# Batch 0's scores in two parts, and loads that cast on GpSimd's queue, in a fused attention and feed-forward kernel

## The chip, the core and the metric

The kernel runs on one core of a Trainium2 chip, as one program with one launch. The metric is the device time of that core in microseconds (us); smaller is better. A core has a matmul engine (TensorE, PE in the profile, whose weight loads are listed apart as PEld), VectorE (DVE), ScalarE (ACT), GpSimd (POOL), and a sync engine (SP) that issues DMAs. Transfers are issued here from SP's queue and from GpSimd's queue. In the built kernels, each queue gives its DMAs eight completion semaphores in turn: the ninth DMA of a queue waits at its issue until the first has landed, the tenth until the second has, and so on.

## The reference

Attention with a selective bias over 8 batches of 8 heads, 576 positions and 64 values a head, and then a gated feed-forward over the 8 x 576 = 4608 tokens:

```python
scores = np.matmul(q, k.transpose(0, 1, 3, 2)) / sqrt(64)
cum = np.cumsum(np.maximum(s, 0.0), axis=-1)
bias = -(cum[:, :, :, None] - cum[:, :, None, :])
scores = np.where(causal, -1e9, scores + np.minimum(bias, 0.0))
attn = softmax(scores)                  # over the keys
x = (attn @ v).transpose(0, 2, 1, 3).reshape(4608, 512)
g = x @ w_gate                          # 512 x 1536
out = (g * sigmoid(g) * (x @ w_val)) @ w_out
```

All inputs and the output are float32 in HBM; the products are made in bf16.

## The kernel before, in words

**Tiles.** Attention works on half batches of four heads ("hb" 0 to 15). For each, k and q (576 KB each) come in as float32, are cast to bf16, transposed on PE, and copied into `KQ[hb % 2]`, two buffers that two half batches share in turn. Four more rows of `KQ`, the cumulative sums in split precision, come from `HL` by four small DMAs (`aug`, L192); they carry the bias into the score product. A head's scores (five tiles of 128 keys, causal, 1600 columns) go into PSUM, ACT takes their exponential into `pt`, GpSimd sets the diagonal blocks' upper triangle to zero (L391, L396), PE multiplies `pt` with v and a column of ones (L413), DVE divides (L429, L430) into `ot`, and PE's transposes put `ot` into `XT`, the feed-forward's input. V comes in by five DMAs a batch (pieces of 64 numbers, 256 bytes) and is cast into `VT[b % 2]`.

**Feed-forward.** It runs over nine tiles of 512 tokens. A tile has twelve steps of a gate product (L626) and a value product (L641), each four matmuls of 512 columns, and then the down product with `w_out` (L670 in tiles 0 and 1; a seven-product form, L711, from tile 2 on). Tile 0 needs tokens 0 to 511, all of batch 0; tile 1 begins with batch 0's last 64 tokens.

**Order.** The order of the instructions on each engine is written by hand and is the program's order. `first_batch` (L882) puts all of batch 0's attention in front of the feed-forward: eight heads, each with one exponential of 1024 and one of 576 columns, with the preparation of half batch 1 between heads 1 and 2, `av` of heads 0 and 1 after head 6, and the rest after head 7. From then on the feed-forward leads: `ffn_items` yields after each product, n counts these items (1 to 24 are the gate and value products of a tile), `hook` runs extra work at a given n, and `pump` puts attention of the next batch between the items, from n = 6 on in tile 0 (`n0`). A matmul that waits holds up all of PE behind it, and the same holds for every other queue.

**Loads.** SP's queue has s, k and q of half batches 0 and 1, the `aug` copies of half batch 0, V of batch 0 (five DMAs), half batch 2, the `aug` of half batches 2 and 3, half batch 3, V of batch 1, half batches 4 and 5. GpSimd's queue has the `aug` of half batch 1, and the weights, which are cast on the way: `wg`, `wv` in two halves of 768 columns each (first half used by steps 0 to 5 of a tile, second half by steps 6 to 11), and `wo` in two halves. The float32 copies of half batches 2 to 4 and of V of batch 1 are cast on GpSimd (L256, L183). Three float32 buffers each for k and q, and one for V, hold back SP's later loads until they are cast.

Of the kernel before, what the change touches and what calls it, by code (L numbers as in the profile page):

```python
# [12 lines left out]
FP32 = mybir.dt.float32  # L13
# [6 lines left out]
def kernel(  # L20
# [20 lines left out]
    HB = 4  # L41
# [67 lines left out]
    with tc.manual_schedule():  # L109
        loaded = {}  # L110
        SRC = {"q": (q, 0), "k": (k, 1)}
# [53 lines left out]

        def load_v(b, cs):
# [36 lines left out]
        def init_vt(i):  # L203
            nc.gpsimd.memset(VT[i][:, :, :, D : D + 1], 1.0)
            nc.gpsimd.memset(VT[i][64:128, 4, :, 0:D], 0.0)
# [24 lines left out]
        init_vt(0)  # L230
        init_vt(1)
        nc.vector.memset(aug_rows(1, 0), 0.0)
        nc.gpsimd.memset(aug_rows(1, 1), 0.0)
        pads(1)

# [10 lines left out]

        cts = {}
# [100 lines left out]
        scs = {}  # L348

        def score_piece(bh, ci):  # L350
            hb, hh = divmod(bh, HB)
            pair = bh < H
            if ci == 0:
                pts[bh] = PTP[0].tile(
                [128, PTW], BF16, tag="pt", bufs=PTP["bufs"], name="pt"
            )
# [3 lines left out]
            if pair:  # L360
                if ci % 2 == 0:
                    bs = take("w")
                    scs[bh] = bs
                else:
                    bs = scs[bh]
                base = (512, 0, 0, 512)[ci]
            else:
                bs = take()
                base = 0
            o = base  # L370
            n = sum(hi - lo for _, lo, hi in CHUNKS[ci])
            sc = view(bs, 1024 if pair else 512)
# [10 lines left out]
            if not pair or ci % 2 == 1:  # L383
                if pair:
                    c0, W = ((576, 1024), (0, 576))[ci // 2]
                else:
                    c0, W = CHUNK_PT[ci], n
                nc.scalar.activation(pt[:, c0 : c0 + W], sc[:, 0:W], AF.Exp, scale=0.125)  # L388
                give(bs)
            if ci == (1 if pair else 0):  # L390
                nc.gpsimd.affine_select(  # L391
                    pt[:, 1088:1600], pt[:, 1088:1600], pattern=[[0, 4], [1, 128]],
                    compare_op=ALU.is_ge, fill=zreg, base=0, channel_multiplier=-1,
                )
# [86 lines left out]
        def side(h, step, ci):  # L481
            bh = HB * h + step
            if bh == H + 3 and ci == 1:
                for c in range(5):
                    cast_v(1, c, nc.gpsimd)
# [60 lines left out]
        def attn_items():  # L546
            for kk in range(H, BH + 2):
                h, step = divmod(kk, HB)
                if kk < BH:
                    if step == 0:  # L550
                        do_later(NR * 2)
                    if step == 1 and 3 < h + 1 < NPE:
                        cast_one(h + 1, "k", nc.gpsimd)
                        cast_one(h + 1, "q", nc.gpsimd)
# [297 lines left out]
        cast_half(0, "k", 0, nc.scalar)  # L852
        cast_half(0, "q", 0, nc.scalar)
        aug(0, SP4)
        load_v(0, range(5))
        load_qk(2)
        for nm in ("k", "q"):
            for g in range(2):
                pe_transpose_half(0, nm, g, 0)
        pe_out(0, "k", 0, 0, nc.scalar)  # L860
        pe_out(0, "k", 1, 0, nc.scalar)
        pe_out(0, "q", 0, 0, nc.vector)
        pe_out(0, "q", 1, 0, nc.vector)
        cast_half(0, "k", 1, nc.scalar)
        cast_half(0, "q", 1, nc.gpsimd)
        aug(1, GP4)
        for nm, eng in (("k", nc.scalar), ("q", nc.vector)):
            for g in range(2):
                pe_transpose_half(0, nm, g, 1)
                pe_out(0, nm, g, 1, eng)  # L870
        cast_one(1, "k", nc.vector)
        cast_one(1, "q", nc.vector)

# [8 lines left out]
        def first_batch():  # L882
            wq = {1: (("g", 0), ("v", 0)), 4: (("g", 1),), 5: (("v", 1),)}
            tail = {
                6: ("a0", "a1"),
                7: ("a2", "a3", "a4", "x0", "a5", "x1", "a6", "a7", "x2", "w6", "x3", "w8"),
            }
            for h in range(H):
                for ci in range(4):
                    score_piece(h, ci)  # L890
# [110 lines left out]
```

## Time and profile before

| | us |
|---|---|
| device time, median of 3 runs (lowest to highest) | 382.94 (382.88 to 384.01) |
| the profiled execution, its own time | 383.17 |
| span from its first to its last instruction | 381.3 |
| first matmul of the feed-forward (L626) | 32.03 |
| first matmul of the down product (L670) | 62.0 |
| PE, weight loads, DVE, ACT, POOL busy | 363.5, 230.5, 289.6, 242.7, 205.9 |
| DMA: hardware-made descriptors (SP's queue), software-made (GpSimd's) | 46.15 MB in 91248 packets, 17.53 MB in 9440 |

The page has the busy share of each engine, the span in 40 slices, the DMA queues and the costliest groups of instructions. Views of the trace give the instructions in order of time, the waits, the groups with each shape apart, the time from a DMA's issue to its landing, and busy time and transfer rate in a chosen stretch. A group of matmuls ends with the modelled latency of its last one, so a step is best read from one start to the next: four matmuls of 512 columns take 0.86 us that way (32.03 to 32.89 in the order of time).

### The profile page before, as it was taken

The numbers are of one execution on the slowest core, as the hardware profiler recorded it, in microseconds if no ns is written. First come the engines' busy times: TensorE is split into PE (matmuls) and PEld (weight loads), VectorE is DVE, ScalarE is ACT, GpSimd is POOL, SyncE is SP. The second block draws the span as 40 slices with busy tenths as digits, with TensorE's granted clock in tenths as the row PEclk, the third lists the DMA queues.
The fourth block names the chain that finished last, engine by engine and source line by source line (L and its number), as shares of the span: only waits on it lengthen the run. The fifth ranks groups of instructions, "written<-read, shape, count | busy, mean of one in ns | idle before, by whom it ended". The sixth has DMA issues, their size and how long they took to land. (4 is left out here: it accounts for less than half of the span.)

```text
span 381.3 us, 8674 instructions
## 1 busy us (share of the span) xinstructions
PE 363.5 (95%) x3246; PEld 230.5 (60%) x3246; DVE 289.6 (76%) x577; ACT 242.7 (64%) x459; POOL 205.9 (54%) x326
## 2 busy tenths in 40 slices
PE   3779999998999999999999999999999999999995
PEld 3666556655555555865586558655875575476464
DVE  8666787456895799868986899589958866975983
ACT  8586788676977786578767876697455523323321
POOL 6684357545364636595458647775665426315220
PEclk9999999999999999999999999999999999999999
DMA  7999999997477998498739965987223213002003
GB/s 234 197 253 263 198 242 268 348 259 162 163 167 246 236 285 220 105 287 216 194 114 285 270 149 158 252 179 166 37 80 101 32 19 127 0 2 97 14 2 110
DMA packets 100729, 64.22 MB, mean 168 GB/s; under 512 B 81888, under 2 KB 85824, under 8 KB 100688
## 3 DMA queue, kind: packets, MB, share of 16 engines
q1 hardware_dynamic: 91248, 46.15, 48.6%
q0 software_dynamic: 9440, 17.53, 17.7%
q8 instruction: 25, 0.41, 0.4%
q14 instruction: 16, 0.13, 0.1%
HBM read 37.90 MB, written 19.86 MB: 151 GB/s over the span
## 5 line engine op out<-in xcount | busy, mean ns | idle before, releaser
L388 ACT ACTIVATE pt<-bank 128x512 bf16<-128x512 f32 x224 | 106.7, 506 | 26.5 <-PE bank L375 18.3
L626 PE MATMUL bank<-XT,wg 128*128 128x512 bf16 x432 | 110.9, 379 | 0.6 <-DVE pp L633 0.2
L641 PE MATMUL bank<-XT,wv 128*128 128x512 bf16 x432 | 110.8, 379 | 0.2
L631 ACT ACTIVATE th<-bank 128x512 bf16<-128x512 f32 x108 | 64.7, 599 | 60.0 <-PE bank L626 54.7
L633 DVE SCALAR_TENSOR_TENSOR pp<-th,bank 128x512 bf16<-128x512 bf16 x108 | 73.9, 684 | 30.2 <-ACT th L631 29.5
L649 DVE SCALAR_TENSOR_TENSOR ht<-pp,bank 128x512 bf16<-128x512 bf16 x108 | 74.1, 686 | 10.3 <-POOL ht L658 0.5
L658 POOL TENSOR_TENSOR ht<-ht 128x512 bf16<-128x512 bf16 x35 | 40.4, 1154 | 53.9 <-DVE su L656 53.8
L375 PE MATMUL bank<-kq 128*128 128x128 bf16 (+4 forms) x504 | 67.5, 240 | 1.6 <-DVE kq L284 1.1
L375 PEld LDWEIGHTS <-kq 128*128 128x128 bf16 x576 | 46.7, 99 | 34.8 <-issue 5.7
L641 PEld LDWEIGHTS <-wv 128*128 128x128 bf16 x432 | 38.6, 98 | 35.8 <-issue 0.4
L626 PEld LDWEIGHTS <-wg 128*128 128x128 bf16 x432 | 38.5, 98 | 35.2 <-issue 1.2
L391 POOL TENSOR_SCALAR_AFFINE_SELECT pt<-pt 128x512 bf16<-128x512 bf16 x64 | 41.8, 653 | 28.5 <-ACT pt L388 28.1
L413 PEld LDWEIGHTS <-pt 128*128 128x128 bf16 x960 | 41.1, 98 | 16.0
L413 PE MATMUL bank<-vt,pt 128*128 128x65 bf16 x840 | 41.8, 194 | 0.0
L447 POOL DMA_DIRECT2D xs<-ot x24 | 21.9, 912 | 31.7 <-DVE ot L430 31.7
L711 PEld LDWEIGHTS <-ht 128*128 128x128 bf16 x336 | 31.2, 98 | 4.3
L197 POOL DMA_DIRECT2D kq<-HL x52 | 31.2, 602 | 0.1
L430 DVE TENSOR_TENSOR ot<-bank,rc 128x320 bf16<-128x320 f32 x56 | 27.5, 492 | 1.9
L396 POOL TENSOR_SCALAR_AFFINE_SELECT pt<-pt 128x64 bf16<-128x64 bf16 x64 | 16.7, 261 | 18.9 <-ACT pt L388 18.7
L711 PEld LDWEIGHTS <-su 128*128 128x128 bf16 x252 | 23.6, 98 | 3.3
L670 PE MATMUL bank<-wo,ht 128*128 128x512 bf16 x96 | 24.6, 379 | 0.0
L775 POOL TENSOR_TENSOR ysb<-ysb 128x512 f32<-128x512 f32 x12 | 15.2, 1271 | 15.3 <-DVE ysb L770 15.3
(96 smaller groups left out, 396.9 us busy)
## 6 DMA issues: line engine op xcount, KB each, us to landing
rawk<-in_k_dram SPq DMA_DIRECT2D x15, 576.0 KB
rawq<-in_q_dram SPq DMA_DIRECT2D x15, 576.0 KB
rawv<-in_v_dram SPq DMA_DIRECT2D x32, 256.0 KB
out_dram<-ysb POOLq DMA_DIRECT2D x32, 256.0 KB, 3.8
xs<-ot POOLq DMA_DIRECT2D x24, 160.0 KB, 3.7
ks<-ck SPq DMA_DIRECT2D x11, 288.0 KB
qs<-cq SPq DMA_DIRECT2D x11, 288.0 KB
wg<-in_moe_w_gate_dram POOLq DMA_DIRECT2D x2, 768.0 KB, 12.6
```

The costliest lines, as they stand in the source:

```text
L197: engs[hh].dma_start(KQ[hb % 2][r][r0 : r0 + 4, :, e * S : (e + 1) * S], HL[bh : bh + 1, :, :, :],)
L375: nc.tensor.matmul(sc[:, o : o + w], T[:, 1, e * S + 128 * tj : e * S + 128 * (tj + 1)], T[:, 0, e * S + lo : e * S + hi], start=True, sto ...
L388: nc.scalar.activation(pt[:, c0 : c0 + W], sc[:, 0:W], AF.Exp, scale=0.125)
L391: nc.gpsimd.affine_select(pt[:, 1088:1600], pt[:, 1088:1600], pattern=[[0, 4], [1, 128]], compare_op=ALU.is_ge, fill=zreg, base=0, channel ...
L413: nc.tensor.matmul(av[:, bi * (D + 1) : (bi + 1) * (D + 1)], pt[:, c0 : c0 + 128], VT[b % 2][:, tj, h, :], start=(tj == 0), stop=(tj == bi),)
L626: nc.tensor.matmul(pg, WG[j][:, c, f0 : f0 + 128], xt[:, c, :], start=(c == 0), stop=(c == 3),)
L631: nc.scalar.activation(th, pg, AF.Tanh, scale=0.5)
L633: nc.vector.scalar_tensor_tensor(pp, in0=th, scalar=1.0, in1=pg, op0=ALU.add, op1=ALU.mult)
L641: nc.tensor.matmul(pv, WV[j][:, c, f0 : f0 + 128], xt[:, c, :], start=(c == 0), stop=(c == 3),)
L649: nc.vector.scalar_tensor_tensor(hp[:, 2 * k2 : 2 * k2 + 2, :].rearrange("p a n -> p (a n)"), in0=pp, scalar=0.5, in1=pv, op0=ALU.mult, op ...
L658: (nc.vector if ft == NFT - 1 else nc.gpsimd).tensor_sub(hp[:, 1:3, :], hp[:, 1:4:2, :], hp[:, 0:3:2, :])
L711: nc.tensor.matmul(ps, lhs(p), rhs(p), start=(first and p == 0), stop=(last and p == NP - 1), skip_group_check=True,)
```

## The change

- The exponentials in front of the feed-forward cover the first 512 queries only: per head 1280 columns, two exponentials of 640 (`score_first`), with one mask of four diagonal blocks (`mask_first`), ten instead of fifteen matmuls in `av_first`, four instead of five transposes in `x_first`.
- The last 64 queries of batch 0 (five matmuls of 64 columns and one exponential of 320 columns a head, `score_tail`) are run by `hook` after items 1 to 8 of tile 0; a mask on GpSimd follows every second head; `av_tail` for heads 0 to 3 comes after item 6, for heads 4 to 7 after item 10; `x_tail` after item 12.
- k and q of half batches 2, 3 and 4, V of batch 1, and three of the five chunks of V of batch 0 are loaded with a cast, straight into the bf16 tiles, by DMAs on GpSimd's queue. Each k or q load becomes two DMAs of 1152 pieces of 64 numbers; the casts on GpSimd fall away, and so do SP's loads of the same data.
- The `aug` of half batch 0 moves from SP's to GpSimd's queue, that of half batch 1 from GpSimd's to SP's. Some memsets change their engine.
- Half batch 0's second rows of k and q are copied on DVE, after scores of heads 0 and 1 have been issued; half batch 1 is cast on GpSimd instead of DVE, and its copies come in two parts.
- 36 matmuls on the identity matrix stand at the start of PE's order.
- `wg` and `wv` second halves are issued in `hook` 1 and 2, `wo` in 11 and 15; attention of batch 1 starts at n = 12 instead of 6, and the preparation of half batch 2 goes from items 1 to 4 to items 9 to 12.

On GpSimd's queue, the order after the last mask of the first batch is thus: four DMAs of half batch 2, `wg` second half, mask of heads 0 and 1, `wv` second half, mask of heads 2 and 3, four DMAs of half batch 3, mask of heads 4 and 5, two memsets of `VT[1]`, five DMAs of V of batch 1, mask of heads 6 and 7, `wo` first half, the masks of heads 8 and 9 with `wo` second half among them, mask of head 10, four DMAs of half batch 4. On SP's queue the `aug` of half batches 2 and 3 is followed at once by V of batch 2 and half batches 5 and 6.

```diff
+        def load_cast(hb):
+            b, g = divmod(hb, 2)
+            for name in ("k", "q"):
+                cts[name, hb] = cp.tile([128, J, NR, D], BF16, tag="c" + name, bufs=2, name="c" + name)
+                for r in range(NR):
+                    nc.gpsimd.dma_start(
+                        cts[name, hb][:, :, r, :],
+                        SRC[name][0][b, g * HB + 2 * r : g * HB + 2 * r + 2, :, :].rearrange(
+                            "e (p j) d -> (e p) j d", j=J
+                        ),
+                    )
+
+        def load_v_cast(b, cs):
+            for c in cs:
+                n = 128 if c < 4 else TAIL
+                nc.gpsimd.dma_start(
+                    VT[b % 2][0:n, c, :, 0:D],
+                    v[b, :, c * 128 : c * 128 + n, :].rearrange("h p d -> p h d"),
+                )
+
...
-        def init_vt(i):
-            nc.gpsimd.memset(VT[i][:, :, :, D : D + 1], 1.0)
-            nc.gpsimd.memset(VT[i][64:128, 4, :, 0:D], 0.0)
+
+        def init_vt(i, eng):
+            eng.memset(VT[i][:, :, :, D : D + 1], 1.0)
+            eng.memset(VT[i][64:128, 4, :, 0:D], 0.0)
 
...
         pads(0)
-        init_vt(0)
-        init_vt(1)
-        nc.vector.memset(aug_rows(1, 0), 0.0)
+        nc.gpsimd.memset(aug_rows(1, 0), 0.0)
         nc.gpsimd.memset(aug_rows(1, 1), 0.0)
         pads(1)
+        init_vt(0, nc.vector)
 
...
+        W1 = 640
+        FIRST_CHUNKS = [
+            [(0, 0, 384), (1, 128, 256), (1, 256, 384)],
+            [(0, 384, 512), (2, 256, 512), (1, 384, 512), (3, 384, 512)],
+        ]
+
+        def first_col(tj, bi):
+            if bi < 3 or tj > 1:
+                return (0, 256, 512, 768)[tj] + 128 * bi
+            return W1 + 384 * tj
+
+        def score_first(bh, half):
+            hb, hh = divmod(bh, HB)
+            if half == 0:
+                pts[bh] = PTP[0].tile([128, 2 * W1], BF16, tag="pt", bufs=8, name="pt")
+            r, e = divmod(hh, 2)
+            T = KQ[hb % 2][r]
+            bs = take("w")
+            sc = view(bs, 1024)
+            o = 0
+            for (tj, lo, hi) in FIRST_CHUNKS[half]:
+                nc.tensor.matmul(
+                    sc[:, o : o + hi - lo],
+                    T[:, 1, e * S + 128 * tj : e * S + 128 * (tj + 1)],
+                    T[:, 0, e * S + lo : e * S + hi],
+                    start=True,
+                    stop=True,
+                )
+                o += hi - lo
+            nc.scalar.activation(
+                pts[bh][:, half * W1 : (half + 1) * W1], sc[:, 0:W1], AF.Exp, scale=0.125
+            )
+            give(bs)
+
...
+        def score_tail(bh):
+            hb, hh = divmod(bh, HB)
+            pr, e2 = divmod(bh, 2)
+            if e2 == 0:
+                tls[pr] = PTP[0].tile([128, 3, TT // 2], BF16, tag="su", bufs=NFT // 2, name="su")
+            r, e = divmod(hh, 2)
+            T = KQ[hb % 2][r]
+            bs = take()
+            sc = view(bs, NCH * 64)
+            for tj in range(NCH):
+                nc.tensor.matmul(
+                    sc[:, tj * 64 : (tj + 1) * 64],
+                    T[:, 1, e * S + 128 * tj : e * S + 128 * (tj + 1)],
+                    T[:, 0, e * S + 512 : e * S + S],
+                    start=True,
+                    stop=True,
+                )
+            tl = tail_view(pr)
+            nc.scalar.activation(
+                tl[:, e2].rearrange("p c n -> p (c n)"), sc, AF.Exp, scale=0.125
+            )
+            give(bs)
+            if e2 == 1:
+                nc.gpsimd.affine_select(
+                    tl[:, :, 4, :], tl[:, :, 4, :], pattern=[[0, 2], [1, 64]],
+                    compare_op=ALU.is_ge, fill=zreg, base=0, channel_multiplier=-1,
+                )
+
+        def av_tail(g):
+            if g == 0:
+                ots["tail"] = otp.tile([128, NCH, 2 * D], BF16, tag="ot", name="ot")
+            bs = take()
+            av = view(bs, 4 * (D + 1))
+            for i in range(4):
+                h = 4 * g + i
+                tl = tail_view(h // 2)
+                for tj in range(NCH):
+                    nc.tensor.matmul(
+                        av[0:64, i * (D + 1) : (i + 1) * (D + 1)],
+                        tl[:, h % 2, tj, :],
+                        VT[0][:, tj, h, :],
+                        start=(tj == 0),
+                        stop=(tj == NCH - 1),
+                    )
+            av3 = av[0:64].rearrange("p (c d) -> p c d", d=D + 1)
+            rc = small.tile([128, NCH], FP32, tag="rc", name="rc")
+            nc.vector.reciprocal(rc[0:64, 0:4], av3[:, :, D])
+            nc.vector.tensor_mul(
+                ots["tail"][0:64, 2 * g : 2 * g + 2, :].rearrange("p a (e d) -> p (a e) d", e=2),
+                av3[:, :, 0:D],
+                rc[0:64, 0:4, None].to_broadcast([64, 4, D]),
+            )
+            give(bs)
+
...
-            if bh == H + 3 and ci == 1:
-                for c in range(5):
-                    cast_v(1, c, nc.gpsimd)
...
-                    if step == 1 and 3 < h + 1 < NPE:
-                        cast_one(h + 1, "k", nc.gpsimd)
-                        cast_one(h + 1, "q", nc.gpsimd)
...
+        keep_warm(36)
+        cast_half(0, "k", 0, nc.scalar)
+        cast_half(0, "q", 0, nc.scalar)
+        aug(0, GP4)
+        aug(1, SP4)
+        load_v(0, (0, 1))
+        for nm in ("k", "q"):
+            for g in range(2):
+                pe_transpose_half(0, nm, g, 0)
+        pe_out(0, "k", 0, 0, nc.scalar)
+        pe_out(0, "k", 1, 0, nc.vector)
+        pe_out(0, "q", 0, 0, nc.vector)
+        pe_out(0, "q", 1, 0, nc.scalar)
+        cast_half(0, "k", 1, nc.scalar)
+        cast_half(0, "q", 1, nc.gpsimd)
+        load_v_cast(0, (2, 3))
+
+        def second_rows(nm):
+            for g in range(2):
+                pe_transpose_half(0, nm, g, 1)
+                pe_out(0, nm, g, 1, nc.vector)
+
+        score_first(0, 0)
+        score_first(0, 1)
+        second_rows("k")
+        score_first(1, 0)
+        second_rows("q")
+        score_first(1, 1)
+        cast_one(1, "k", nc.gpsimd)
+        cast_one(1, "q", nc.gpsimd)
+        w_load("g", 0)
+        mask_first(0)
+        score_first(2, 0)
+        score_first(2, 1)
+        for g in range(2):
+            pe_transpose(1, "k", g)
+            pe_out(1, "k", g, 0, nc.vector)
+        cast_v(0, 0, nc.gpsimd)
+        w_load("v", 0)
+        mask_first(1)
+        cast_v(0, 1, nc.gpsimd)
+        mask_first(2)
+        score_first(3, 0)
+        score_first(3, 1)
+        mask_first(3)
+        for g in range(2):
+            pe_transpose(1, "q", g)
+            pe_out(1, "q", g, 0, nc.vector)
+        for nm in ("k", "q"):
+            for g in range(2):
+                pe_out(1, nm, g, 1, nc.vector)
+        for h in range(4, 7):
+            score_first(h, 0)
+            score_first(h, 1)
+            mask_first(h)
+        load_v_cast(0, (4,))
+        av_first(0)
+        score_first(7, 0)
+        av_first(1)
+        score_first(7, 1)
+        mask_first(7)
+        load_cast(2)
+        av_first(2)
+        av_first(3)
+        x_first(0)
+        av_first(4)
+        x_first(1)
+        av_first(5)
+        av_first(6)
+        x_first(2)
+        av_first(7)
+        keep_warm(6)
+        x_first(3)
+        keep_warm(8)
...
-        hook = {
-            1: [lambda: prep_one(2, 0)],
-            2: [lambda: prep_one(2, 1)],
-            3: [lambda: prep_one(2, 2)],
-            4: [lambda: prep_one(2, 3)],
-            6: [lambda: cast_one(3, "k", nc.gpsimd), lambda: cast_one(3, "q", nc.gpsimd)],
-        }
+        hook = {n: [] for n in range(1, 37)}
+        for bh in range(H):
+            hook[1 + bh].append(lambda bh=bh: score_tail(bh))
+        hook[1].append(lambda: w_load("g", 1))
+        hook[2].append(lambda: w_load("v", 1))
+        hook[4].append(lambda: aug(2, SP4))
+        hook[5].append(lambda: load_cast(3))
+        hook[6].append(lambda: av_tail(0))
+        hook[7].append(lambda: init_vt(1, nc.gpsimd))
+        hook[7].append(lambda: load_v_cast(1, range(5)))
+        hook[8].append(lambda: aug(3, SP4))
+        hook[10].append(lambda: av_tail(1))
+        hook[12].append(x_tail)
+        for i in range(4):
+            hook[9 + i].append(lambda i=i: prep_one(2, i))
+        hook[11].append(lambda: w_load("o", 0))
+        hook[15].append(lambda: w_load("o", 1))
+        hook[18].append(lambda: load_cast(4))
+        hook[20].append(lambda: load_qk(5))
...
-            n0 = 6 if tt == 0 else 0
+            n0 = 12 if tt == 0 else 0
```

## What I predict

> **What bounds the kernel now.** I read the page's busy shares and slices first, then PE's waits after the feed-forward's start, then the order of time of the first 33 us, the groups with shapes apart, and last the transfers: rates by stretch, landings, and SP's own order.
>
> ```profile
> PE 363.5 (95%) x3246; PEld 230.5 (60%) x3246; DVE 289.6 (76%) x577; ACT 242.7 (64%) x459; POOL 205.9 (54%) x326
> ...
> PE bank L375 <- DVE kq L284: 1.1, 1, 1.1
> PE bank L375 <- DVE ht L649: 0.5, 2, 0.3
> PE bank L626 <- DVE pp L633: 0.2, 1, 0.2
> PE bank L626 <- ACT XT L468: 0.2, 1, 0.2
> ```
>
> The last four are all that PE waited for after 32 us: from there PE is the bound, so a matmul added there costs its full time, and so does any wait. Before that, PE waits, mostly on ACT and DVE:
>
> ```profile
> 11.15 1.51 PE L375 MATMUL wide<-kq 128*128 128x128 bf16 x9 [0.57 <-DMA kq<-HL]
> ...
> L388 ACT ACTIVATE pt<-wide 128x1024 bf16<-128x1024 f32 x8 | 8.2, 1024 | 4.6 <-PE wide L375 3.9
> L388 ACT ACTIVATE pt<-wide 128x576 bf16<-128x576 f32 x8 | 5.2, 644 | 0.0
> ...
> L326 DVE COPY kq<-one 64x640 bf16<-64x640 bf16 x6 | 4.8, 818 | 3.3 <-ACT pt L388 2.3 <-PE one L311 1.0
> L326 DVE COPY kq<-one 64x512 bf16<-64x512 bf16 x6 | 4.1, 710 | 0.0
> ...
> 30.23 0.49 DVE L430 TENSOR_TENSOR ot<-one,rc 128x320 bf16<-128x320 f32 x1
> ...
> 32.03 1.02 PE L626 MATMUL bank<-XT,wg 128*128 128x512 bf16 x4 [0.17 <-ACT XT L468]
> ```
>
> First score at 11.15, exponentials to 27.39 (21.61 + 5.78 in the order of time), DVE's divisions to 30.72, then transpose and copy, feed-forward at 32.03. The third thing to see is the DMA engines' load, and what small pieces cost:
>
> ```profile
> 12.00:14.00 2.00, 1.37 (x10) 0.95 (x9) 1.13 (x2) 1.56 (x2) 0.68 (x2) 1.00 0.96 218
> 42.00:44.00 2.00, 2.00 (x12) 0.95 (x11) 0.64 (x2) 1.90 (x4) 0.49 (x1) 1.00 1.21 198
> 56.00:58.00 2.00, 2.00 (x37) 1.41 (x34) 1.01 (x2) 1.23 (x4) 2.00 (x6) 1.00 1.03 399
> ...
> 27.89 24.55 SPq L172 DMA_DIRECT2D rawv<-in_v_dram  x5
> ```
>
> The last two numbers of a stretch are DMA share and GB/s. At 12 to 14 us, V's 256-byte pieces fill the engines at 218 GB/s; at 56 to 58, k and q rows of 2304 bytes fill them at 399. At 42 to 44, V shares them with `wo`, and SP needs 24.55 us to issue the five V loads of batch 1.
>
> **What the Trainium skill says.** "DMA: Bandwidth & Descriptors", Specifications, gives 512 bytes as the smallest transfer for line rate; the trace agrees (218 against 399 GB/s). The same page, SWDGE vs HWDGE vs iDMA, has casts only on GpSimd's queue, and each DMA engine going round robin between the queues; the trace agrees: V beside weights took 6.8 to 7.3 us an issue, about 1.05 alone. "TensorE: Matmul & The Clock Gate", Part 1, has PE at half clock until about 3.4 us of activity, and again after such a window of idleness. The trace: nine transposes from 5.40 take 1.17 us, five from 32.89 take 0.44. Taking off the last one's 0.31 and 0.22 us leaves steps of 107 and 55 ns.
>
> **The change, part by part.** The sum is made against the profiled execution (383.17, span 381.3), 0.23 above the median 382.94; I apply it to the median.
>
> *Front.* (a) First score: the copies of `HL` need DVE's chain (ends 7.82), which starts up to 0.7 earlier without the 1.07 us memset. They now go by GpSimd, where such copies landed 1.9 to 3.4 us after issue, the first at about 11.3; loads of half batch 1 fill the engines until about 10.7. I take 11.0 (9.8 to 11.4). (b) An exponential of 640 columns, between 576 and 1024: 644 + 64 x 380/448 = 698 ns; two are 1.40 us a head instead of 1.67, 2.2 us less over eight. (c) But twelve copies of rows (four of half batch 0, eight of half batch 1), 0.77 us each, now follow the first scores on DVE: 12.2 + 9.2 = 21.4, and about a microsecond of bubbles, since transposes stand behind scores. Head 6 waits for the last: 22.5 + four exponentials 2.8 + 0.3 = 25.6 against 27.39. (d) Six divisions follow, 0.62 each (0.68 now; 256 instead of 320 columns), from 24.7: 28.4. Transpose and copy take 1.3 as now: feed-forward at 29.7, gain 2.3. With both ends of (a) and one microsecond either way on (c): 1.2 to 3.5. The 36 dummy matmuls (107 ns: 3.9 us) lie in PE's idle time before 5.40 and cost nothing; a warmer clock is in the range.
>
> *PE work moved behind 29.7.* 40 score and 40 value matmuls at 30 ns (45 matmuls from 25.98 take 1.52, less the last one's 0.19, over 44) and four transposes at 55: 2.6 us, all exposed. So the front alone is worth +0.3: nothing.
>
> *Casts taken away.* On GpSimd six of 1.14, five of 0.61 and two more: 9 us, but PE waited for none. Nothing (±0.3).
>
> *Loads moved, and the queue behind them.* GpSimd's last mask of the first batch ends near 26.3. A DMA of 1152 pieces is not in the trace; issues there cost 0.55 (128 pieces), 0.78 (512), 0.91 (640): I take 1.05 (0.8 to 1.3). Half batch 2: 26.3 to 30.5. `wg`, a mask, `wv`: 32.4. The next mask needs the exponential of head 3's last queries, after item 4: 29.7 + 4 x 1.01 (0.86 and 0.15 of scores) + 0.5 = 34.3. Half batch 3: 34.6 to 38.8; mask and memsets 40.1; four V DMAs 44.1. The fifth V DMA is the eighth since half batch 3's first, so it waits for that one's landing. By transfer: a half batch of pieces, 4608, as V's 1.18 MB at 210 GB/s is 5.7 us (before 2.95 at 399). A weight half 4.0: the first two landed at 26.7 and 30.7 (16.2 + 10.5, 17.0 + 13.7). So half batch 2 is through at 33.2, `wg` 37.2, `wv` 41.2, and half batch 3's first quarter at 42.6; it has landed at 44.2 (1.6, estimated from the copies of `HL`), or 45.6 where SP's loads alternate with it. Then V's fifth issue 0.9 and the mask of heads 6 and 7, 0.3: 45.4 to 46.8. PE wants this mask after item 10: 29.7 + 8.6 + tails 1.2 + first `av_tail` 0.6 + transposes 0.3 = 40.4. **PE waits 5.0 to 6.4 us.** Behind it stand all of the tile's remaining products. Such a gap may also cool PE's clock (the skill's Part 1): at most 1.7 us, which the next wait would cover.
>
> *What is late next.* SP's queue, rid of 13 loads, comes early to V of batch 2 and half batches 5 and 6: 5.7 + 2 x 2.95 = 11.6 us of transfers near 41, just when GpSimd's queue has 5.7 (half batch 3), 5.7 (V) and 2 x 4.4 (`wo`; landings 47.2 and 52.5, less V's share) to come. `wo`'s second half lands at 41.2 + 20.2 + 1.6 = 63.0 if SP's loads come last, at 74.6 if they all come first. PE wants it after 24 items (20.7), tails 2.6, 36 transposes 2.0, five heads of scores 3.5, two heads of values 0.9, half a down group 1.3: 29.7 + 31.0 = 60.7. So the delay of tile 0 in all lies between 5 (the mask alone; it covers the 2.3 here) and 13.9; the middle is 9.4. Slack before was some 9 us: `wo` landed at 52.5 and was wanted at 62.0. What is moved later in the tile (attention from n = 12) only packs ACT, 64% busy, more densely: 0 (-0.5 to +1).
>
> Sum: 382.94 - 2.3 + 2.6 + 9.4 = **392.6**.
>
> **Rivals.**
> *Mask wait only* (388.2): SP's loads stay behind, as they did while the first weights filled the engines, and only GpSimd's queue holds PE: -2.3 + 2.6 + 5.0. For: half batch 3, issued by SP at 26.89 behind `wg` and `wv`, came so late that its cast on GpSimd began at 35.85. Against: from 42 to 44 V took its turns beside `wo`.
> *Faster* (380.5): the front gains 5 (warm PE, early `HL` copies, no half batch 2 in front), and GpSimd's queue keeps ahead: -5.0 + 2.6. It decides if the mask of heads 6 and 7 is done within 13 us of the mask that ends the first batch. For: GpSimd is only 54% busy over the span, and casts leave it. Against: 15.1 us of transfers lie ahead of the landing that the mask hangs on.
> *Even* (383): the same queue holds PE for less than 1 us, since pieces that are written as 128 bytes go at twice V's rate.
> *Small writes slow* (403): a piece read as 256 and written as 128 bytes takes half as long again as V's; two half batches and V, 17 us, become 25.5, nearly all of it falls on PE, and half batch 4, wanted soon after, adds 2.
>
> **How the numbers follow.** Forecast 0.50 (its own range 389.5 to 397.5), mask only 0.22, faster 0.12, even 0.06, slow writes 0.10. A measurement of this kernel tells 0.3%, 1.15 us, from no change. Faster 0.12, same 0.06, slower 0.82. Leaving out the faster case and the upper part of the slow one, 0.2 in all: 382 to 400.
>
> **What would show it.** Feed-forward's first matmul near 29.7; `pt` exponentials near 700 ns; PE idle 5 to 6 us before the second `av_tail`, released by the mask on GpSimd; GpSimd's V issue held by a DMA's landing; PE waiting again for half batch 3's transposes or `wo`; DMA share over 1 from 27 to 70 us at near 200 GB/s. Wrong if the mask comes by 40, if GpSimd's DMAs take far less than 0.8 or more than 1.3 us, if cast pieces move faster than 210 GB/s of what is read, or if the feed-forward starts before 28.

## The result, and the profile after

The changed kernel takes 401.22 us (median of 4 runs, 398.43 to 401.55); the kernel before took 382.91 beside it. The ratio is 1.0461, with a 95% interval of 1.0406 to 1.0515: slower by 18.3 us, where 9.7 were forecast, and just above the range, which ended at 400. The profiled execution took 401.47 us, with a span of 399.2. The page of the changed kernel has PE 9.5 us busier than before (363.5), and shows in its row of clocks three places, from 10 to 30, 50 to 60 and 80 to 90, where less than full speed was granted (`PEclk`, in tenths, one digit for 10 us). In the row of before every digit is a 9, but its record of the clock begins only at 16.74; until then its matmuls take the steps of half clock (107 ns, where they take 55 later), so the front of before was not at full clock either:

```profile
PE 373.0 (93%) x3306; PEld 236.2 (59%) x3306; DVE 289.1 (72%) x580; ACT 242.4 (61%) x466; POOL 216.6 (54%) x331
...
PEclk9689979989999999999999999999999999999998
```

PE's waits in the changed kernel (us in total, times, longest): the last three are new and all lie in tile 0.

```profile
PE wide L388 <- DMA kq<-HL: 4.9, 1, 4.9
PE bank L488 <- POOL su L474: 3.9, 1, 3.9
...
PE bank L816 <- DMA wo<-in_moe_w_out_dram: 1.7, 1, 1.7
...
PE bank L316 <- DMA ck<-in_k_dram: 1.4, 1, 1.4
```

The order of time of PE in the changed kernel (start, us, and in brackets the idle time before). Lines two and three are the same seven score matmuls of another head: 1.22 us and 0.74, half clock and full clock. The feed-forward starts at 33.60 (32.03 before).

```profile
6.86 0.85 PE L330 MATMUL one<-ident,cq 128*64 128x128 bf16 x9 [0.28 <-ACT cq L283]
12.59 1.22 PE L388 MATMUL wide<-kq 128*128 128x384 bf16 x7 [4.88 <-DMA kq<-HL]
...
17.79 0.74 PE L388 MATMUL wide<-kq 128*128 128x384 bf16 x7 [0.48 <-DVE kq L345]
...
33.60 1.02 PE L772 MATMUL bank<-XT,wg 128*128 128x512 bf16 x4 [0.23 <-ACT XT L441]
```

GpSimd's order of time shows why the mask of heads 6 and 7 (L474) is late, and what comes behind it: five V loads in front of it, each near 0.9 us of issue, one of them held by a landing; `wo`'s second half is issued only at 60.87.

```profile
43.66 2.67 POOL L182 DMA_DIRECT2D vt<-in_v_dram  x3
47.03 1.68 POOL L182 DMA_DIRECT2D vt<-in_v_dram  x2 [0.71 <-DMA wv<-in_moe_w_val_dram]
48.77 0.29 POOL L474 TENSOR_SCALAR_AFFINE_SELECT su<-su 128x128 bf16<-128x128 bf16 x1
50.37 0.85 POOL L361 DMA_DIRECT2D wo<-in_moe_w_out_dram  x1 [1.31 <-DMA ck<-in_k_dram]
...
60.87 0.84 POOL L361 DMA_DIRECT2D wo<-in_moe_w_out_dram  x1
```

The stretches of the changed kernel (length, PE busy, granted clock, DMA share, GB/s) show what tile 0 goes through: PE nearly idle while the DMA share, the time of all packets over that of the 16 engines, is near 2 (44 to 49 and 73 to 78), and in between PE busy at half clock.

```profile
44.00:49.00 5.00, 1.25 (x18) 0.92 2.01 163
49.00:55.00 6.00, 5.89 (x32) 0.50 1.61 208
73.00:78.00 5.00, 1.89 (x14) 1.00 1.99 175
```

Where the 18.3 us of the two profiled executions lie: 1.6 in front of the feed-forward; 15.4 in tile 0, which takes 63.2 us from the first gate product to that of tile 1 (47.8 before); 1.3 later and outside the span. Of the 15.4, PE's own work is 2.4 to 2.5 (its matmuls at full-clock steps sum to some 48.2 us, 45.8 before), and 13.0 is lost time (15.0 against 2.0): the wait for the mask 4.0, for `wo` 1.9, for half batch 4 1.6, for a copy 0.8 (these start to start, so a little more than the waits above), and the half clock at 49 to 55 and 79 to 82 some 4.7 together (3.1 and 1.6).

### The profile page after: what moved, and what is told of

Read it like the earlier page. It is cut to its first block, busy times and chain, and to the rows that moved or that the text cites. A ratio compares the mean times of both kernels' runs of the same rounds, so it can differ in the third digit from the quotient of the medians.

```text
span 399.2 us, 8816 instructions
## 1 busy us (share of the span) xinstructions
PE 373.0 (93%) x3306; PEld 236.2 (59%) x3306; DVE 289.1 (72%) x580; ACT 242.4 (61%) x466; POOL 216.6 (54%) x331
## 5 line engine op out<-in xcount | busy, mean ns | idle before, releaser
L779 DVE SCALAR_TENSOR_TENSOR pp<-th,bank 128x512 bf16<-128x512 bf16 x108 | 73.8, 683 | 32.6 <-ACT th L777 31.8
L795 DVE SCALAR_TENSOR_TENSOR ht<-pp,bank 128x512 bf16<-128x512 bf16 x108 | 74.0, 686 | 11.6 <-PE bank L787 1.0
L531 PEld LDWEIGHTS <-kq 128*128 128x128 bf16 x504 | 40.7, 98 | 27.6 <-DVE kq L303 1.2
L543 POOL TENSOR_SCALAR_AFFINE_SELECT pt<-pt 128x512 bf16<-128x512 bf16 x56 | 36.9, 658 | 32.0 <-ACT pt L540 31.8
L565 PEld LDWEIGHTS <-pt 128*128 128x128 bf16 x840 | 37.6, 98 | 16.1 <-issue 0.5
L816 PE MATMUL bank<-wo,ht 128*128 128x512 bf16 x96 | 25.8, 390 | 1.7 <-DMA wo<-in_moe_w_out_dram 1.7
L548 POOL TENSOR_SCALAR_AFFINE_SELECT pt<-pt 128x64 bf16<-128x64 bf16 x56 | 14.7, 263 | 15.2 <-ACT pt L540 15.1
```

Source lines behind the costliest of these rows:

```text
L531: nc.tensor.matmul(sc[:, o : o + w], T[:, 1, e * S + 128 * tj : e * S + 128 * (tj + 1)], T[:, 0, e * S + lo : e * S + hi], start=True, sto ...
L543: nc.gpsimd.affine_select(pt[:, 1088:1600], pt[:, 1088:1600], pattern=[[0, 4], [1, 128]], compare_op=ALU.is_ge, fill=zreg, base=0, channel ...
L565: nc.tensor.matmul(av[:, bi * (D + 1) : (bi + 1) * (D + 1)], pt[:, c0 : c0 + 128], VT[b % 2][:, tj, h, :], start=(tj == 0), stop=(tj == bi),)
L779: nc.vector.scalar_tensor_tensor(pp, in0=th, scalar=1.0, in1=pg, op0=ALU.add, op1=ALU.mult)
L795: nc.vector.scalar_tensor_tensor(hp[:, 2 * k2 : 2 * k2 + 2, :].rearrange("p a n -> p (a n)"), in0=pp, scalar=0.5, in1=pv, op0=ALU.mult, op ...
```

## The experiments

| run | what is different | median us | ratio to before (95%) | feed-forward | tile 1 |
|---|---|---|---|---|---|
| before | | 382.9 | | 32.0 | 79.8 |
| after | the change | 401.2 | 1.046 (1.041 to 1.052) | 33.6 | 96.8 |
| a_aug_back | `aug` queues as before | 399.6 | 1.042 (1.039 to 1.045) | 32.1 | 95.3 |
| a_warm | dummies in two gaps of PE | 399.7 | 1.044 (1.041 to 1.046) | 32.1 | 95.0 |
| a_mask_first | V loads behind the mask | 400.5 | 1.048 (1.043 to 1.053) | 31.8 | 95.5 |
| a_old_loads | the split, old loads | 389.4 | 1.017 (1.014 to 1.020) | 32.6 | 84.9 |
| a_sp_late | SP's later loads held | 394.0 | 1.028 (1.027 to 1.030) | 32.0 | 89.7 |
| a_rows | k and q cast in whole rows | 395.7 | 1.033 (1.029 to 1.036) | 32.0 | 92.5 |
| a_three | three repairs at once | 388.9 | 1.015 (1.013 to 1.017) | 32.0 | 84.9 |
| a_four, a_five | and 40, 64 dummies in front | 388.2, 388.3 | 1.014, 1.016 | 32.0, 30.9 | 85.1, 84.4 |
| b_cast_loads | before, with the loads alone | 403.8 | 1.054 (1.051 to 1.057) | 36.4 | 99.2 |
| b_warm | before, with dummies in front | 383.0 | 1.0005 (0.9991 to 1.0019) | 30.9 | 79.4 |
| b_front | and `wo`'s second half later | 383.4 | 1.0013 (1.0006 to 1.0021) | 32.7 | 80.5 |

The last two columns are the starts of the first gate product and of tile 1 in each profiled execution. Dummies are matmuls on the identity matrix whose result nothing reads; they only keep PE busy.

**One wait at a time.** Three runs each repair one thing that PE was seen to wait for.

```diff
-        aug(0, GP4)
-        aug(1, SP4)
+        aug(0, SP4)
...
+        aug(1, GP4)
```

> The changed kernel with the four small copies of half batch 0's cumulative sums on SP's queue and those of half batch 1 on GpSimd's, as in the kernel before. Theory (the front is late because the first score waits for copies that GpSimd issues late and that land late): first score at 11.1 to 11.4 instead of 12.59, last exponential ends 1.2 to 1.5 earlier (27.3 to 27.6 instead of 28.74), feed-forward starts near 32.2 instead of 33.60, time near 400 (1.2 to 1.5 less than 401.2), since what follows is held by PE and loads that move along. Rival (the front is bound by DVE's twelve copies of rows, not by its start): first score earlier, but the last exponential within 0.5 of 28.74, and no gain. Rival (tile 0 is bound by GpSimd's queue from the first batch on): feed-forward 1.4 earlier, but the wait before the second av_tail grows by as much, time unchanged within 0.5.

```diff
+        keep_warm(78, "w")
         score_first(0, 0)
...
+        hook[10].append(lambda: keep_warm(66))
         hook[10].append(lambda: av_tail(1))
```

> The changed kernel with 78 matmuls on the identity matrix ahead of the first score and 66 ahead of the second av_tail, so that PE works in its two longest gaps (7.7 to 12.6, and 44.6 to 49.1). Theory (the gaps halve PE's clock afterwards and that costs 2.5 us at 49 to 55, and some of the front's time): full clock from 49 on, tile 0 2.0 to 2.8 us shorter, 398.5 to 399.3; if transposes and scores of the front are held by PE's slow clock from 12.6 to 17.5 too, another 0.5 to 1.5 less. Rival (what is late next takes the gain: the second half of the output weights is bound by transfers): the wait before the first down product grows from 1.9 to about 4, and time falls by less than 0.7. Rival (the low clock has another cause than idleness): clock in 50 to 55 stays near 0.5, time same or slower.

```diff
-        hook[7].append(lambda: init_vt(1, nc.gpsimd))
-        hook[7].append(lambda: load_v_cast(1, range(5)))
+        hook[9].append(lambda: init_vt(1, nc.gpsimd))
+        hook[9].append(lambda: load_v_cast(1, range(5)))
```

> The changed kernel with the memsets of VT[1] and the five V loads of batch 1 moved on GpSimd's queue behind the mask of heads 6 and 7 (after item 9 instead of item 7). Theory (the mask waits only for its place behind the V loads): mask near 43 to 44, wait before the second av_tail below 1 us instead of 4.0, no half clock at 49 to 55 (2.5), time 394 to 396 if the output weights come as before or a little later. Rival (GpSimd's queue is bound by transfers in sum, so the wait moves): the mask comes early, but the first down product or half batch 4 waits 4 us and more, time 399 to 401. Rival (only the wait goes, the clock halves anyway): 397 to 398.

All three did locally what they should, and none moved the time by more than 1.7 us, which is less than the changed kernel's own runs differ (398.4 to 401.6). In a_aug_back the first score came at 11.03, but the feed-forward began at 32.06, and three runs that keep the changed kernel's front (a_mask_first, a_sp_late, a_rows) began it at 31.8 to 32.0: this run doesn't show that the copies' queue cost the feed-forward anything. In a_warm dummies kept PE busy through the gap and its clock stayed full until 73.6; in a_mask_first the mask was done by 41.7 and its wait was gone. But PE then waits for transfers in a_mask_first:

```profile
PE bank L816 <- DMA wo<-in_moe_w_out_dram: 6.6, 2, 4.1
...
PE bank L316 <- DMA ck<-in_k_dram: 1.7, 1, 1.7
```

In a_warm the wait for `wo` grew to 3.3. PE's wait for half batch 4 ended at 77.9 in the changed kernel and at 75.8, 75.5 and 76.5 in these three. Counted from the start of the feed-forward, that is 44.3, 43.7, 43.5 and 44.7 us, although a_aug_back still had the mask's wait, of 3.4, a_warm had filled it with dummies, and a_mask_first had none. The order of time of the changed kernel, and below it that of a_mask_first, shows that earlier issues did not help either:

```profile
60.87 0.84 POOL L361 DMA_DIRECT2D wo<-in_moe_w_out_dram  x1
75.86 0.59 PE L816 MATMUL bank<-wo,ht 128*128 128x512 bf16 x2 [1.71 <-DMA wo<-in_moe_w_out_dram]
77.89 0.44 PE L316 MATMUL bank<-ident,ck 128*128 128x128 bf16 x5 [1.40 <-DMA ck<-in_k_dram]
...
53.49 0.84 POOL L361 DMA_DIRECT2D wo<-in_moe_w_out_dram  x1
73.70 1.01 PE L816 MATMUL bank<-wo,ht 128*128 128x512 bf16 x2 [4.11 <-DMA wo<-in_moe_w_out_dram]
76.50 0.69 PE L316 MATMUL bank<-ident,ck 128*128 128x128 bf16 x5 [1.74 <-DMA ck<-in_k_dram]
```

GpSimd issued `wo`'s second half and the first load of half batch 4 each 7.4 us earlier there, and PE got them only 2.2 and 1.4 us earlier. So landings set the end of tile 0, and the waits ahead of them only divide the time up: the rivals "what is late next" and "the wait moves" hold.

**Whose transfers.** On SP's queue V of batch 2 and half batches 5 and 6 go out from 43 to 60 beside GpSimd's V, `wo` and half batch 4. A write of DVE to half batch 5's buffer, after item 21, holds them back, and V of batch 2 is put behind half batch 5:

```diff
-        hook[20].append(lambda: load_qk(5))
+        def late_loads():
+            t = raw.tile([128, NR, J, D], FP32, tag="rawk", name="rawk")
+            nc.vector.memset(t[0:1, 0, 0, 0:2], 0.0)
...
+        hook[21].append(late_loads)
```

> The changed kernel with SP's loads of half batch 5 and V of batch 2 (and half batch 6 behind them) held until DVE has run what stands after item 21 of tile 0 (near 60 us), where they were issued from 43 to 60. Theory (all transfers share one rate, 37.5 us of them from 40 to 77.5, and SP's 11.6 us take their turns ahead of the output weights and half batch 4): the weights' second half and half batch 4 come some 8 to 11 us earlier, so the waits of 1.9 and 1.5 us and the half clock at 79 to 82 (1.6) go, the mask wait of 4.0 stays or shrinks by up to 1; time 395.5 to 397. Rival (GpSimd's order of instructions, not the rate, makes them late): the second half of the output weights is still issued near 60 and lands after 70, time 399.5 to 401.5. Rival (the held loads come too late themselves): new waits for half batch 5 near 75 to 95, time over 401.

```diff
+                t = t.rearrange("x j r d -> x (j r d)").rearrange("x (r n) -> x r n", r=NR)
...
-                            "e (p j) d -> (e p) j d", j=J
+                            "e (p j) d -> (e p) (j d)", j=J
```

> The changed kernel with k and q of half batches 2 to 4 still cast on GpSimd's queue, but in whole rows: 128 pieces of 2304 bytes a DMA instead of 1152 of 256. PE then needs two transposes of 64 rows where it had one of 128, 18 more for each half batch, 54 in all (some 3 us of PE's time at 55 ns). Theory (the pieces are the price: a half batch takes 5.7 us of transfer instead of some 3, and 4.0 us of GpSimd's issues instead of some 2.2): mask of heads 6 and 7 at 45 or before, half batch 4 landed near 68 instead of 77.9, waits of tile 0 from 7.3 to below 2.5 us, time 392 to 396 with the 3 us of transposes in it. Rival (the queue and the alternation with SP's loads are the price, whatever the pieces): half batch 4 lands after 74, time 399 to 403.

Held so, they went out from 67.0 on, and PE did not wait for them. That took 7.2 us off, more than the theory's 5, and left no wait for `wo` or half batch 4. The stretches of a_sp_late show room where the changed kernel had none:

```profile
48.00:54.00 6.00, 5.87 (x30) 0.61 2.32 151
54.00:58.00 4.00, 3.95 (x36) 1.00 0.45 73
58.00:62.00 4.00, 3.35 (x27) 1.00 0.41 53
```

`wo`'s second half was issued at 58.51 there and landed 8.7 us later; in the changed kernel it took 15.0 us from its issue at 60.87, and 20.2 from 53.49 in a_mask_first. So it was the rate and not GpSimd's order that made it late. The packets say the same: from 48 to 52 the changed kernel moved 1644 packets of GpSimd's queue beside 1697 of SP's; almost alone (24 of SP's), from 44 to 48 in a_sp_late, GpSimd's moved 4702 in as long. The Trainium skill ("DMA: Bandwidth & Descriptors", SWDGE vs HWDGE vs iDMA) says that each DMA engine goes round robin between the two kinds of queue; one to one is what is seen. The mask's wait stayed, at 3.0: that one is GpSimd's order, with the five V issues taking 4.23 us in a row.

Whole rows took 5.5 us off, although PE had 54 transposes more. A DMA of 128 rows costs GpSimd half of the issue, as its order of time in a_rows shows (2.0 us for two in the changed kernel):

```profile
37.03 1.10 POOL L174 DMA_DIRECT2D ck<-in_k_dram  x2
38.11 1.08 POOL L174 DMA_DIRECT2D cq<-in_q_dram  x2
...
44.82 1.58 POOL L184 DMA_DIRECT2D vt<-in_v_dram  x2 [1.88 <-DMA wv<-in_moe_w_val_dram]
```

The mask came at 46.45, where the theory had 45 or before, since the time saved was spent in the wait for `wv`'s landing, and PE still waited 2.9 for it; half batch 4 made PE wait 0.7 and `wo` not at all. Half batch 4 landed at 73.4 to 76.0, near the rival's 74 and not at the theory's 68. So each of the two, the pieces and SP's company, is part of the price, as either repair alone left 12.8 or 11.1 us of the loss; no run has both.

**All three, and the split by itself.**

> Three repairs at once: small copies of half batch 0 on SP's queue, V loads of batch 1 behind the mask of heads 6 and 7, and SP's loads of half batch 5 and V of batch 2 held until item 21 of tile 0. Theory (each repair alone only hands the wait on, as they gave 1.6, 0.7 and what the run beside this one gives; together they free tile 0): no wait over 1.5 us in tile 0, full clock from 33 on, tile 0 near 51.5 to 53, time 387 to 390, the sum 401.2 - 1.4 - 6.5 - 5.0 = 388.3. Rival (the bytes of GpSimd's queue are themselves too many before the first down product): waits for the output weights or half batch 4 stay over 3 us, time 393 to 397.

(The edits of a_aug_back, a_mask_first and a_sp_late together.)

> The changed kernel's split scores with the loads as before: k and q of half batches 2 to 4, V of batches 0 and 1 as float32 on SP's queue and casts on GpSimd and VectorE; weights, queues of the small copies and the split stay. Theory (the loads make the waits of tile 0, the split costs PE 2.5 us and the front): mask wait below 1 us, no wait for the output weights over 1 us, no half clock after 33, tile 0 near 50.5 (47.8 + 2.5) instead of 63.2, feed-forward start 33 to 34.5, time 386 to 389. Rival (the split itself makes the waits, since scores and masks of the tails stand in the way): mask wait stays 3 to 4 us, time 396 to 400. Rival (split is worth something by itself, below the kernel before): below 382.

```diff
-        load_v(0, (0, 1))
+        load_v(0, range(5))
+        load_qk(2)
...
-        hook[5].append(lambda: load_cast(3))
+        hook[5].append(lambda: cast_one(3, "k", nc.gpsimd))
+        hook[5].append(lambda: cast_one(3, "q", nc.gpsimd))
```

> The kernel before with the loads alone changed: k and q of half batches 2 to 4, V of batch 1 and three chunks of V of batch 0 by DMAs with cast on GpSimd's queue, no split of the scores. Theory (two parts, the loads worth some 12 us of the 18.3 and the split 6.5, but the mask wait of 4 us and its 2.5 of half clock exist only with both): 384 to 390, PE waiting for the output weights before the first down product, none for a mask. Rival (the loads alone carry the loss): 394 to 397. Rival (the loads are free where nothing of the split waits behind them): 382 to 384.

```diff
-                    load_qk(3)
-                    load_v(1, range(5))
-                    load_qk(4)
-                    cast_one(2, "k", nc.gpsimd)
-                    cast_one(2, "q", nc.gpsimd)
+                    load_cast(2)
+                    load_cast(3)
+                    load_v_cast(1, range(5))
...
-                        cast_one(h + 1, "k", nc.gpsimd)
-                        cast_one(h + 1, "q", nc.gpsimd)
+                        load_cast(h + 1)
```

Together the repairs gave 12.3 us, where singly they gave 1.7, 0.7 and 7.2. PE's waits in a_three no longer have a transfer among them after the first score; what is left in tile 0 are copies on DVE:

```profile
PE bank L531 <- DVE kq L345: 1.3, 1, 1.3
...
PE bank L772 <- DVE kq L345: 0.5, 1, 0.5
```

a_old_loads ends at the same time: the loads, once repaired, cost no more than the old ones in this kernel. What stays, 6.4 us in a_old_loads and 5.7 in a_three against the runs of before that stood beside each, belongs to the rest of the change: the split, and with it the new front and the later order of tile 0, which no run takes apart. Tile 0 takes 52.3 us in a_old_loads and 52.9 in a_three against 47.8: 2.5 of PE work, and 2.1 and 2.5 in waits over 0.4 us each, for the copies of half batch 2's preparation, now packed into items 9 to 12.

b_cast_loads fell outside the theory and both rivals: 403.8, worse than with the split. PE's waits there are of another kind:

```profile
PE bank L316 <- DMA ck<-in_k_dram: 8.2, 2, 6.1
...
PE one L432 <- DMA vt<-in_v_dram: 4.6, 1, 4.6
```

With preparation of half batch 2 still at items 1 to 4, PE meets its landing 6 us early, and the values of batch 0 wait for V in front. So the parts do not add up. That the change's later preparation covers some of what its loads cost is a reading of these waits: no run moved the preparation alone, and this run also puts half batches 2 and 3 and V of batch 1 in one row on GpSimd's queue ahead of `wo`.

**The front.** PE idles from 7.7 to 12.6 before the first score, and its clock is at half from 10.65 to 17.48. The kernel before is at half until 16.74, so the 36 dummies at the start brought little by themselves: the full clock that followed them, from 7.24 to 10.65, met only 0.47 us of work.

> The run with three repairs (388.9) with 40 more matmuls on the identity matrix before the first score, so that PE does not idle from 7.7 to 11.2. Theory (PE's half clock in the front is what keeps the split from starting the feed-forward early): last exponential at 25.6 to 26.2, feed-forward at 30.3 to 30.9 instead of 31.99, time 387.3 to 387.9. Rival (DVE's twelve copies bound the front): feed-forward after 31.6, time within 0.5 of 388.9. Rival (the front's gain is taken by the next wait in tile 0): feed-forward near 30.5, but tile 1 starts within 0.4 of 84.9.

> As the run with three repairs (388.9) with 64 instead of 40 matmuls on the identity matrix before the first score; with 40 PE still idled from 9.3 to 11.6 and its clock fell to half from 12 to 15.5 and again from 22.7 to 26. Theory (with PE busy until the first score the clock stays full, DVE's copies start 1.2 us earlier against the first score, and no second half-clock stretch holds the values and scores of heads 0, 1 and 7): last exponential 14.0 to 14.4 after the first score, as in the run with 78 (13.14 to 27.18), so 25.4 to 26.0, feed-forward 30.2 to 30.9, time 387 to 388. Rival (dummies delay the first score as much as they save, since it needs only the copies of the sums): first score after 12.2, feed-forward 31.5 or later, time within 0.6 of 388.9. Rival (front earlier, but tile 0 hands it on): feed-forward below 31, tile 1 starts within 0.4 of 84.9.

```diff
+        keep_warm(40, "w")
         score_first(0, 0)
```

(64 in a_five.) a_four doesn't answer the question: its 40 dummies ended at 9.3, the first score came at 11.62, and the clock fell all the same (0.58 at 12 to 14). With 64, PE had 0.2 us of idleness, and its stretches in a_five read:

```profile
12.00:14.00 2.00, 1.87 (x25) 1.00 1.13 245
...
18.00:20.00 2.00, 0.69 (x8) 1.00 0.86 151
20.00:22.00 2.00, 0.94 (x9) 0.88 1.16 210
22.00:24.00 2.00, 1.82 (x18) 0.50 1.16 209
```

First score 11.16, last of DVE's twelve copies 22.13, last exponential 26.08, feed-forward 30.94: 1.05 earlier than in a_three. The last exponential is just past the theory's 25.4 to 26.0; from 21.5 to 24.9 the clock was at half again. Only 0.6 of it was left at tile 1, and the time, 388.3 against 388.9 with overlapping runs, doesn't tell the two apart.

**A version that beats both?**

> The kernel before with 36 matmuls on the identity matrix at the start of PE's order and 44 more before the first score, nothing else changed. Theory (PE's half clock until 16.7 delays the first two heads' scores and the transposes of half batch 1, and ACT idles 3.9 us for them): last exponential 1 to 2 us earlier than 27.39, feed-forward near 30.5, time 381 to 382. Rival (ACT and DVE bound the front, PE's clock does not matter there): within 0.3 of 382.95. Rival (the extra matmuls delay the first transposes or scores): first score after 11.5, time 383.3 to 384.5.

> The kernel before with 36 matmuls on the identity matrix at the start of PE's order, 18 before the first score (44 held it until 12.0 in the earlier run), and the second half of the output weights issued at item 8 of tile 0 instead of with the first, so that V of batch 1 and half batch 4 share the transfers with 4.4 us less before 56 us. Theory (the gain of 1.1 in front was eaten by GpSimd's cast of half batch 4, which stands behind V's late landings): feed-forward at 30.2 to 30.6, no wait for that cast, time 381.3 to 382.2. Rival (something else of tile 0 is as late): 382.5 to 383.3. Rival (the weights' second half now comes after 61): over 383.5.

```diff
+        keep_warm(36)
         cast_half(0, "k", 0, nc.scalar)
...
-                    w_load("o", 1)
...
+            8: [lambda: w_load("o", 1)],
...
+        keep_warm(18, "w")
         first_batch()
```

(44 instead of 18 in b_warm, and `wo` as before.) No. b_warm brought the feed-forward forward by 1.08 us in its profiled execution and lost 0.6 of it again in tile 0 (48.4 us against 47.8), where PE waited 0.5 for GpSimd's cast of half batch 4; tile 1 started only 0.4 earlier. In b_front that wait was gone, but the first score came at 11.9, PE's clock fell to half from 19.5 to 26.3, and the feed-forward started at 32.73. Neither beats the kernel before.

## Why the prediction was wrong

The direction and most of the mechanism in tile 0 were right; two terms of the sum were mis-sized, and they make 7.5 of the 8.6 us missing.

*The front*, forecast at -2.3, measured +1.6, so 3.9 off. Its working was short at every step:

| step | forecast, us | changed kernel | other runs with the split |
|---|---|---|---|
| (a) to the first score | 11.0 | 12.59 | 11.5 to 12.3 with the same front (a_mask_first, a_sp_late, a_rows); 11.0 to 11.6 with the copies on SP's queue (a_aug_back, a_three, a_four, a_five) |
| (c) on to the end of the twelve copies | 11.5 | 12.08 | 11.0 where the clock was full (a_warm, and a_five up to 21.5), 12.1 in a_aug_back, a_mask_first, a_rows and a_three |
| (c) on to the last exponential's end | 3.1 | 4.07 | 3.1 where the clock did not fall a second time in the front (a_warm, a_mask_first, a_sp_late), 3.6 to 4.1 otherwise |
| (d) on to the feed-forward | 4.1 | 4.86 | 4.85 to 4.87 in all nine |

In (a), GpSimd's copies landed 2.8 to 4.1 us after their issue, where 1.9 to 3.4 was taken. In (c), the clock was not priced: "a warmer clock is in the range" looked at the dummies before 5.40 and not at PE's idleness after 7.7. In (d), the lengths were right (exponentials 698 ns forecast, 702 measured; a division 0.62 forecast, 0.18 + 0.42 measured), but six divisions were lined up without a wait from 0.9 us before the last exponential's end. They began 0.4 before it and took 4.1 us instead of 3.7, since DVE waited for PE before two of them:

```profile
30.32 0.18 DVE L426 RECIPROCAL rc<-one 128x4 f32<-128x4 f32 x1 [0.25 <-PE one L414]
...
31.83 0.18 DVE L426 RECIPROCAL rc<-one 128x4 f32<-128x4 f32 x1 [0.32 <-PE one L414]
```

Over the four executions of this front the feed-forward started at 31.8, 32.0, 32.0 and 33.6, never before 31.8, so the stated gain of 1.2 to 3.5 was not there in any; but 1.6 to 1.8 of the 3.9 belong to this one execution, which was later than the other three. How much of that comes from the first copy's landing (11.4 to 12.5 in the four) and how much from the clock's second fall stays open.

*Tile 0*, forecast at +9.4 of waits, measured +13.0. The step that failed stands under *What is late next*: of a delay between 5 and 13.9, "the middle is 9.4". The bounds were good, the middle was not. The upper end was that of SP's loads going first; SP issued them in a row from 43.4 to 60.2, and PE's wait for `wo` ended at 75.86 against the 74.6 worked out for that order. a_sp_late shows that this choice decides: 7.2 us. The wait for half batch 4 (1.6) stood only under the rival of slow small writes, and the wait for a copy (0.8) nowhere.

Right, by the runs: PE work 2.6 (2.4 to 2.5); GpSimd's issue 1.05 (1.00); the mask's wait 5.0 to 6.4 (4.0, as the mask was later by about 3 and PE, at 45.1 against 40.4, by 4.7). V's issue was held by a landing, but it was the fourth, by `wv`, and not the fifth, by half batch 3. That the casts taken off GpSimd are worth nothing was not tested alone; they add up to 9.9 us before the "two more", not 9. The cooled clock was priced at no more than 1.7, which is half of 3.4 us; it stayed at half for 6.8, from 48.2 to 55.0, and cost 3.1. a_warm showed it covered by the next wait, as forecast: with full clock there, tile 0 was 0.2 us shorter.

The rival *small writes slow* came near the time (403), but by luck and not by its mechanism: written as 128 bytes, the pieces go at 1175 a microsecond when almost alone (4702 in 4 us), faster than V's of 256 bytes in the kernel before (218 GB/s, some 850). At 256 bytes read for each, that is some 300 GB/s of what is read, so one of the forecast's signs of being wrong, more than 210, did come, and the rival *even* had part of this right. Beside SP's loads the rate was some 410 (1644 in 4 us). The slow rival's last clause, half batch 4, was what happened. Of the remaining 1.3 us, 0.4 came between the start of tile 1 and PE's last matmul, 0.5 after that matmul and 0.4 outside the span; their cause is open.

## What to carry to other kernels

When loads move off a queue, ask what that queue does next: its later loads start early and take every second packet from those wanted soon, and holding them back was worth more here (7.2 us) than any other single repair (0.7 to 5.5). When a chain of transfers sets the end of a stage, repairing PE's waits one by one gives next to nothing; look for a landing that stays put while the waits before it change. And a gap of PE is priced with what its clock does afterwards, unless a later wait covers that, as it did in a_warm.

## What the runs showed of the hardware

PE's clock fell not only after whole idleness: in a_five it fell at 21.5 with PE busy for 1.51 of the 3.41 us before, in b_front at 19.5 with 1.80. In a_mask_first a stretch as long with 1.67 (18.84 to 22.25) was followed by no fall, so no threshold of PE's busy time can be read from these traces. The changes come on a grid: in the changed kernel at 7.24, 10.65, 17.48, 24.31, 27.72, 48.20, 55.03, 78.92 and 82.33, each 3.41 us, or a multiple of it, after the one before. The Trainium skill ("TensorE: Matmul & The Clock Gate", Part 1) calls the window of activity free-running, so that one kernel meets it at different phases; these runs agree: with the same front, a_rows and the changed kernel had a second stretch of half clock before 28, a_mask_first and a_sp_late had none.
